# The last stage of a fused attention and GLU kernel: more output buffers, two kinds of transfers on another queue, one output more added in DRAM

## Chip, core and metric

The kernel runs on one core of a Trainium2 chip. The metric is device time in microseconds: the median of 3 runs before the change is 725.43 us (724.59 to 726.86). All times below are in us unless they say otherwise.

## What is computed

```python
def _A_ref(x, wqkv, wo):                 # x: 1 x 2048 x 640
    q, k, v = ...                        # 32 heads of 20
    phi = lambda t: jnp.where(t > 0, t + 1, jnp.exp(t)) + 1e-6
    pq, pk = phi(q), phi(k)
    kv = jnp.einsum("bhsd,bhse->bhde", pk, v)
    z = jnp.einsum("bhsd->bhd", pk)
    num = jnp.einsum("bhqd,bhde->bhqe", pq, kv)
    den = jnp.einsum("bhqd,bhd->bhq", pq, z)[..., None] + 1e-6
    return (num / den, heads put side by side) @ wo

def _B_ref(x, w_gate, w_up, w_down):     # 640 -> 1536 -> 640
    return (sigmoid(x @ w_gate) * (x @ w_up)) @ w_down

g = sigmoid((x * gate_w).sum(-1, keepdims=True))
out = g * _A_ref(...) + (1 - g) * _B_ref(...)
```

Everything is float32, and the output is written transposed, as `out_t`, 640 x 2048.

## The kernel before

Float32 products are made of three matmuls each: an operand is split into a high part (a ScalarE copy, rounded) and a low part (a VectorE subtraction), and high x high, high x low and low x high are added in PSUM (`prod`, `mm3`, `split`).

Linear attention lets kv and wo be folded into one 640 x 640 matrix **M**. What is left for the last stage is `out_t = M^T . pq`, with pq scaled by g / den in each column, plus b, the GLU part times (1 - g). The stage works on five row blocks of 128 (`o`, 0 to 4) and four column groups of 512 (`g`), in the order 2, 3, 0, 1. Groups 2 and 3 are **stage 0** (`n = 0`), groups 0 and 1 **stage 1** (`n = 1`). For groups 2 and 3 b was written to `out_t` before, so the attention part is added to it by a DMA with an addition, which GpSimd's queue alone issues. For groups 0 and 1 b lies in SBUF (`tb`, `BL`), not yet multiplied by (1 - g).

In each stage there are two `ABlock`s (here block 0 and block 1). One computes two row blocks of both groups with seven products in place of eight, as in Strassen's scheme: steps s1 to s7, emitted in the order s1, s2 of both blocks, the fifth row block by itself (`a_unit`), then s3, s4, s5, s7, s6 of block 0 and the same of block 1. Four of M's sums that a block needs (`MS`) are loaded by `load_ms`: for block 0 into one tile (`ws`), for block 1 into two (`wg`), in eight DMAs. Pre-added inputs are the `pt` tiles, and the corrections for the fifth row of inputs lie in `ws`.

The results leave through buffers that are taken in turn by `st_tile` from the list `ST`. A step copies PSUM into a buffer on ScalarE (c11 in s1, c12 in s3, c22 in s4, one more in s6), VectorE adds a second PSUM tile to it (c11 after s2, c22 after s5, c12 after s7), and a DMA writes or adds it to `out_t`. The `ch` PSUM tile of a block goes through s1, s3, s5 and s6; s3 is copied out and s5 goes on adding in the same tile. `ST` has six buffers before: columns 2 and 3 of `fac`, one `wu` tile, `tt` (a tile of the tag `t`), `OMG[2]`, `tt`. A buffer comes round at the seventh call; then the copy waits for the DMA that read it.

What fixes the order: `Order` is a planner that runs while the program is built. It keeps estimates of when TensorE, ScalarE and VectorE are done, and places work waiting in its lists between the matmuls when it fits. Its result is a fixed order on each engine. `Ring` (`sp` for SyncE's queue, `gp` for GpSimd's) estimates DMA landings for it and issues them. On the chip each engine goes through its own list in order; GpSimd and SyncE each use eight semaphores in turn for their DMAs, so the ninth waits for the first to land.

`queue_b_scale(g, os_, store)` multiplies rows of b by (1 - g); rows in `store` are then written to `out_t`, and the attention part is added to them by `more` later. Rows not stored are added up in SBUF by `to_b` and written once. `acc` says which of a block's two rows go by `more`: (c12 and s6's) and (c22).

Of the kernel before, what the change touches and what calls it, by code (L numbers as in the profile page):

```python
# [10 lines left out]
OP = mybir.AluOpType  # L11
# [338 lines left out]
class Ring:  # L350
# [16 lines left out]
    def dma_start(self, out, src, **kw):  # L367
        o = self.order
        start = max(self.t, o.data(out, [src]))
        self.t = start + self.issue  # L370
        (r1, n), (r2, _) = (self.run(ap, 0 if getattr(ap.tensor, "_space", DRAM) == DRAM else 1) for ap in (out, src))
        r = min(r1, r2)
        took = 1.25 * max(1, n // r) * (7 + 0.0377 * r) / 16e3
        self.cell = self.rings.issue(self.n, start + self.lag, took)
        o.put(out, [src], self.cell)
        return self.engine.dma_start(out, src, **kw)  # L376

P_LAG, A_LAG, V_LAG = 0.2, 0.18, 0.14

# [7 lines left out]
def gated_mix_kernel(ctx: ExitStack, tc: tile.TileContext, x0, xt, xn, wk, wv, wo, wst_q, wst_f, out_t):  # L387
# [8 lines left out]
    sp, gp = Ring(nc.sync, order, rings, 0, 0.38, 1.5), Ring(nc.gpsimd, order, rings, 1, 0.55, 2.2)  # L396
# [80 lines left out]
    fac = fac_tile()  # L477
# [597 lines left out]
    g = GTBatch(0, [0])  # L1075
# [8 lines left out]
    for c in range(1, 4):  # L1084
        ck = chunks[c]
        if c == 1:
# [14 lines left out]
            g = GTBatch(c, batches[c])  # L1101
# [98 lines left out]
        if c > 1:  # L1200
            g = GTBatch(c, batches[c])
# [53 lines left out]
    def tt(name, dt=F32, shape=(P, TG)):  # L1255
        return pw.tile(list(shape), dt, name=name, tag="t", bufs=4)

    def ct(name, dt=F32, shape=(P, TG)):
        return pw.tile(list(shape), dt, name=name, tag="c", bufs=5)
# [838 lines left out]
    def h_tile(dt=F32R, i=None):  # L2098

        if i is not None:  # L2100
            pass
        elif "h" not in turn:
            i = 0
        else:
            i = (0, 0, 0, 0, 1, 1, 1, 2)[turn["h"] % 8]
            turn["h"] += 1
        pool = pw2 if i == 2 and len(down_pool) < 3 else down_pool[i]
        return pool.tile([P, 2, TG], dt, name="hf", tag=f"hf{i}", bufs=(4, 3, 1)[i])
# [28 lines left out]
    def h_due(p, name):  # L2137
        seg = {"T1": 1, "B22": 1, "T2": 2, "T3": 2, "T4": 3}[name]
        return {"stream": ("h", p), "due": order.due((order_pr[0], 2 * p + 3, 3 if name == "B22" else f"d{seg}"))}
# [15 lines left out]
    def tail_s(f, blk):  # L2155
# [21 lines left out]
        def t5():  # L2177
# [4 lines left out]
            sub(t4, t4, HR[p, "T2"])  # L2182
            HR[p, "T3"] = t3 = HR[p, "B22"]
            b12 = HR.pop((p, "B12"))
# [13 lines left out]
    OMG = {}  # L2198
# [81 lines left out]
    def down_pair(pr, p):  # L2280
# [31 lines left out]
        d.out("Z1", 3, 1)  # L2312
        d.go("X0", "S3", "T3")
        d.out("X0", 1, 1)
        d.go("X1", "S3", "T3", q=1)
        d.out("X1", 3, 1)
# [29 lines left out]
    def down_last(tail):  # L2346
# [43 lines left out]
        d.out("Z1", 3, 1)  # L2390
        d.go("X0", "S3", "T3")
        d.out("X0", 1, 1)
        d.go("X1", "S3", "T3", q=1)
        d.out("X1", 3, 1)
# [308 lines left out]
    q = q_phase(1, lambda k: [(b12h[:, k], b12l[:, k])], extra)  # L2703
# [32 lines left out]
    q = q_phase(0, lambda k: [tuple(t[:, k] for t in b12)], {0: [lambda: next(down), more_c], 1: [lambda: next(down)], 8: [lambda: order.need((nx[1], 6), False), early_omg], 9: [lambda: queue_ds(LAST), lambda: queue_df(LAST)], 10: [lambda: queue_last("T2", "T3", "T4")]})  # L2736
# [3 lines left out]
    PL, PQ, BL, MHL, PT, MS, X3, ST = {}, {}, {}, {}, {}, {}, [], []  # L2740

    def x2_tile(name="pl", dt=F32):
        return px.tile([P, 2, TG], dt, name=name, tag="x2", bufs=10)
# [30 lines left out]
    def load_ms(i):  # L2774

        t = [ws_tile().rearrange("p a b -> p (a b)")] if i == 0 else [wg_tile().rearrange("p a b -> p (a b)") for _ in range(2)]
        n, q = ((4, sp), (2, gp))[i]
        cs = slice(2 * i * P, 2 * (i + 1) * P)
        at = 4 * n * P

        def view(c, k):
            return t[c][:, k * P:(k + 1) * P]
        for c in range(len(t)):
            w = 4 if i == 0 else 1
            for k in range(0, n, w):
                q.dma_start(f32(t[c][:, 4 * k * P:4 * (k + w) * P].rearrange("p (j c) -> p j c", c=2 * P)),
                             ms_dram[:, n * c + k:n * c + k + w].rearrange("p u j c -> p (u j) c")[:, :, cs])
            for k in range(n):
                u = n * c + k
                for h, f in enumerate(("a11", "a21") if u < 2 else ("a12", "a22")):  # L2790
                    MS[i, f, u % 2] = [view(c, 4 * k + 2 * n + h) for n in range(2)]
        room = (t[0][:, at:at + 2 * P], t[1][:, at:at + 2 * P] if i else MS["spare"])
        for e, o in (("u", (1, 2)), ("d", (0, 3))):
            dst = room[e == "u"]
            for k in range(2):
                q.dma_start(f32(dst[:, k * P:(k + 1) * P]), m5_dram[:, o[k], i * P:(i + 1) * P])
            MS[i, e] = [dst[:, k * P:(k + 1) * P] for k in range(2)]
# [139 lines left out]
    def queue_b_scale(g, os_, store=()):  # L2937
        def fn(o):
            vec2(BL[g][o], BL[g][o], OMG[g], OP.mult)
            if o in store:  # L2940
                gp.dma_start(rows(g, o), BL[g][o])
        for o in os_:
            order.add(0, v_cost(TG), lambda o=o: fn(o), ("b", g, o), lambda o=o: b_at(g, o))

    def rows(g, o, c0=0, c1=TG):
        return out_t[o * P:(o + 1) * P, g * TG + c0:g * TG + c1]

    def a_unit(g, o, cuts=(0, TG)):

        os_ = slice(o * P, (o + 1) * P)  # L2950
        if g < 2:
            order.need(("b", g, o))
        dst = BL[g][o] if g < 2 else st_tile()
        for c0, c1 in zip(cuts, cuts[1:]):
            ps = ps_tile("rot") if g > 1 else SEED.pop((g, o, c0) if (g, o, c0) in SEED else (g, o))
            prod(ps[:, c0:c1], [(MHL[k, 0][:, os_], MHL[k, 1][:, os_], PQ[g][k][0][:, c0:c1],
                                 PQ[g][k][1][:, c0:c1]) for k in range(KC)], g > 1)
            if len(cuts) > 2:
                ch = c0 + P if c1 == TG else c1
                vec_copy(dst[:, c0:ch], ps[:, c0:ch], "p")  # L2960
                if ch < c1:
                    act(dst[:, ch:c1], ps[:, ch:c1], AF.Copy, "p")
                    nc.scalar.dma_start(rows(g, o, ch, c1), dst[:, ch:c1])
                sp.dma_start(rows(g, o, c0, ch), dst[:, c0:ch])
                continue
            act(dst, ps, AF.Copy, "p")
            if g > 1:
                gp.dma_start(rows(g, o), dst, accum_op=OP.add)
            else:
                sp.dma_start(rows(g, o), dst)  # L2970

    class ABlock(Block):
        def __init__(self, i, n):
            self.o = (2 * i, 2 * i + 1)
            self.i, self.n, self.at = i, n, 1e9
            self.acc = [n == 0 or i == 0, n == 0 or i == 0]
            self.ga, self.gb = groups[2 * n:2 * n + 2]

        def w(self, i, c):
# [14 lines left out]
        def out(self, j, g, src):  # L2994
            if self.n:
                sp.dma_start(rows(g, self.o[j]), src)
            else:
                gp.dma_start(rows(g, self.o[j]), src, accum_op=OP.add)

        def more(self, j, g, src):  # L3000
            if self.n:
                order.need(("b", g, self.o[j]))
            gp.dma_start(rows(g, self.o[j]), src, accum_op=OP.add)

        def to_b(self, j, g, src, after="p", last=False):

# [104 lines left out]
    for g in range(2):  # L3111
        BL[g] = {o: tb[:, o, g] for o in range(KC)}
    load_ms(0)
    T3 = [h_tile() for _ in range(2)]
    last_down(0, range(2 * KC))
    load_p(0)
    load_p(1)
    ST += [fac[:, 2], fac[:, 3], f32(wu_tile()).rearrange("p a b -> p (a b)")[:, :TG], lambda: tt("st"),
           OMG[2], lambda: tt("st")]
    blocks = [[ABlock(i, n) for i in range(2)] for n in range(2)]  # L3120
    queue_pt(0)
    for b in blocks[0]:
# [16 lines left out]
    def rest(n, hooks={}):  # L3139
        for i in range(2):  # L3140
            for s in (3, 4, 5, 7, 6):
                getattr(blocks[n][i], f"s{s}")()
                for fn in hooks.get((i, s), ()):
                    fn()
                order.fill()
# [6 lines left out]

    def queue_later():

        order.need(("c11", 0))
        for g, o, tag in ((0, 0, "dd"), (0, 2, "dd"), (0, 4, "rot")):
            queue_seed(g, o, tag)
        queue_pt(1)
        queue_b_scale(1, (0, 1), (0, 1))
        queue_b_scale(0, (1,), (1,))  # L3160

    def queue_end():

        order.add(0, 2 * v_cost(TG // 2), seed_parts, ("b", 1, KC - 1))
        queue_b_scale(1, (2, 3))
        queue_b_scale(0, (3,))
    rest(0, {(0, 6): [lambda: load_omg(0), lambda: load_omg(1)], (1, 4): [queue_later]})
    firsts(1)
    for u in range(KC):
        order.need(("pq", 1, u))  # L3170
    rest(1, {(0, 6): [queue_end]})
    order.need("late")
    a_unit(1, KC - 1, (0, TG // 2, TG))
# [40 lines left out]
```

## Time and profile before

| what | value |
|---|---|
| median of 3 runs | 725.43 us (724.59 to 726.86) |
| profiled execution: time, span | 724.84 us, 722.8 us |
| mean TensorE clock granted | 0.997 |
| TensorE busy, 560 to 660 | 100.00 of 100 |
| TensorE busy, 660 to 680 | 18.92 of 20.00 |
| TensorE busy, 680 to 700 | 18.94 of 20.00, clock 0.91 |
| TensorE busy, 700 to 710 | 10.00 of 10.00 |
| TensorE busy, 710 to the end of the span | 9.07 |
| DMA moved over the whole span | 187.03 MB, mean 259 GB/s |

The span is that of the profiled execution, from its first to its last instruction; its own time is 2.0 us more. The profile shows instructions with start, duration and, in brackets, how long the engine stood idle ahead of them and what ended that. Names are those of the tiles without their numbers. In a row of the view by stretches stand the stretch, its length, each engine's busy time with its instructions, the granted clock, the share of time that the 16 DMA engines were busy, and GB/s; a row with one engine's column has that engine's alone. In a row of DMAs stand what moves, the queue, how many, KB each, and the median time from issue to landing. In a row of waits stand the waiter, whom it waited for, the time in all, how often and the longest.

### The profile page before, as it was taken

The numbers are of one execution on the slowest core, as the hardware profiler recorded it, in microseconds if no ns is written. First come the engines' busy times: TensorE is split into PE (matmuls) and PEld (weight loads), VectorE is DVE, ScalarE is ACT, GpSimd is POOL, SyncE is SP. The second block draws the span as 40 slices with busy tenths as digits, with TensorE's granted clock in tenths as the row PEclk, the third lists the DMA queues.
The fourth block names the chain that finished last, engine by engine and source line by source line (L and its number), as shares of the span: only waits on it lengthen the run. The fifth ranks groups of instructions, "written<-read, shape, count | busy, mean of one in ns | idle before, by whom it ended". The sixth has DMA issues, their size and how long they took to land.

```text
span 722.8 us, 10177 instructions
## 1 busy us (share of the span) xinstructions
PE 715.9 (99%) x3386; PEld 604.2 (84%) x3386; DVE 583.1 (81%) x1051; ACT 375.4 (52%) x720; POOL 202.9 (28%) x337
## 2 busy tenths in 40 slices
PE   9999999999999999999999999999999999999897
PEld 8999999888888888878888888888888888888786
DVE  4988878987887889789978887547778878689895
ACT  5764748257656673746465862464333333336351
POOL 0311111113433434343522123023421413514402
PEclk9999999999999999999999999999999999999999
DMA  8474558699885969598979788996988897997836
GB/s 272 121 199 115 174 140 265 145 315 296 311 309 215 350 189 337 183 351 286 321 239 329 244 260 281 332 347 220 352 298 298 288 368 272 356 331 219 186 59 174
DMA packets 74985, 187.03 MB, mean 259 GB/s; under 512 B 13930, under 2 KB 27898, under 8 KB 74166
## 3 DMA queue, kind: packets, MB, share of 16 engines
q1 hardware_dynamic: 45510, 97.41, 40.1%
q0 software_dynamic: 29136, 88.77, 39.6%
q8 instruction: 26, 0.43, 0.2%
q10 hardware_dynamic: 288, 0.23, 0.1%
q14 instruction: 25, 0.20, 0.1%
HBM read 105.01 MB, written 76.38 MB: 251 GB/s over the span
## 4 chain that ended last, share of the span: by engine, by line
PE 93%; DMA 3%; issue 2%; DVE 1%; ACT 1%; POOL 0%; POOLq 0%; ACTq 0%
PE ch L419 10%; PE ch L421 10%; PE ch L420 10%; PE cc L421 7%; PE cc L420 7%; PE cc L419 7%; PE dd L419 6%; PE dd L421 6%; PE dd L420 6%; PE rot L419 5%; PE rot L421 5%; PE rot L420 5%; PE ch L430 4%; PE cc L430 3%; PE dd L430 2%
## 5 line engine op out<-in xcount | busy, mean ns | idle before, releaser
L439 DVE TENSOR_TENSOR hf<-c,hf 128x512 fp32r<-128x512 f32 x77 | 52.4, 688 | 30.7 <-ACT hf L435 30.5
L435 ACT ACTIVATE hf<-c 128x512 fp32r<-128x512 f32 (+1 forms) x79 | 48.7, 625 | 37.8 <-DVE c L439 37.8
L435 ACT ACTIVATE c<-ch 128x512 f32<-128x512 f32 x43 | 25.7, 597 | 78.7 <-PE ch L430 62.5
L439 DVE TENSOR_TENSOR c<-cc,c 128x512 f32<-128x512 f32 x38 | 26.1, 688 | 26.1 <-ACT c L435 15.2
L439 DVE TENSOR_TENSOR tb<-rot,tb 128x512 f32<-128x512 f32 x60 | 39.0, 683 | 2.9 <-PE rot L421 2.9
L419 PE MATMUL ch<-xth,ws 128*128 128x512 f32 x94 | 36.8, 391 | 0.0
L421 PE MATMUL ch<-xth,ws 128*128 128x512 f32 x94 | 36.6, 390 | 0.0
L420 PE MATMUL ch<-xtl,ws 128*128 128x512 f32 x94 | 36.6, 389 | 0.0
L439 DVE TENSOR_TENSOR c<-c,c 128x512 f32<-128x512 f32 x48 | 33.0, 687 | 2.6 <-ACT c L435 2.0
L435 ACT ACTIVATE dd<-ch 128x512 f32<-128x512 f32 x22 | 12.8, 583 | 38.2 <-PE ch L430 38.2
L376 POOL DMA_DIRECT2D b_dram<-tb x24 | 20.4, 945 | 33.2 <-ACT tb L435 32.9
L435 ACT ACTIVATE c<-dd 128x512 f32<-128x512 f32 x21 | 12.5, 596 | 31.8 <-PE dd L430 30.3
L376 POOL DMA_DIRECT2D zacc<-kr x8 | 7.0, 870 | 77.2 <-DVE logit L845 59.4
L439 DVE TENSOR_TENSOR wst<-wst 128x256 f32<-128x256 f32 (+2 forms) x69 | 27.4, 412 | 1.5
L419 PE MATMUL dd<-xrh,wg 128*128 128x512 f32 x62 | 24.5, 395 | 0.0
L439 DVE TENSOR_TENSOR tb<-dd,tb 128x512 f32<-128x512 f32 x32 | 21.9, 685 | 3.0 <-PE dd L421 3.0
L421 PE MATMUL dd<-xrh,wg 128*128 128x512 f32 x62 | 24.2, 390 | 0.0
L420 PE MATMUL dd<-xrl,wg 128*128 128x512 f32 x62 | 24.1, 390 | 0.0
L435 ACT ACTIVATE c<-c 128x512 f32<-128x512 f32 x31 | 19.5, 628 | 8.1 <-DVE c L439 7.9
L419 PE MATMUL cc<-xbh,ws 128*128 128x512 f32 x58 | 22.6, 389 | 0.0
L420 PE MATMUL cc<-xbl,ws 128*128 128x512 f32 x58 | 22.6, 389 | 0.0
L421 PE MATMUL cc<-xbh,ws 128*128 128x512 f32 x58 | 22.6, 389 | 0.0
(807 smaller groups left out, 2539.2 us busy)
## 6 DMA issues: line engine op xcount, KB each, us to landing
wst<-wst_f SPq DMA_DIRECT2D x12, 640.0 KB, 6.8
wf<-wg POOLq DMA_DIRECT2D x12, 640.0 KB, 4.4
wg<-wf SPq DMA_DIRECT2D x12, 640.0 KB, 8.2
b_dram<-tb POOLq DMA_DIRECT2D x24, 256.0 KB, 6.9
xnst<-xn SPq DMA_DIRECT2D x16, 320.0 KB, 4.2
xst<-xt SPq DMA_DIRECT2D x8, 640.0 KB, 5.9
wp<-ws POOLq DMA_DIRECT2D x20, 256.0 KB, 5.8
wp<-ws POOLq DMA_DIRECT2D x10, 512.0 KB, 4.3
```

The source lines that it names most:

```text
L376: return self.engine.dma_start(out, src, **kw)
L419: nc.tensor.matmul(out, l_hi, r_hi, start=first, stop=False, skip_group_check=True)
L420: nc.tensor.matmul(out, l_hi, r_lo, start=False, stop=False, skip_group_check=True)
L421: nc.tensor.matmul(out, l_lo, r_hi, start=False, stop=last, skip_group_check=True)
L430: nc.tensor.matmul(out, w, x, start=False, stop=n == len(singles) - 1, skip_group_check=True)
L435: nc.scalar.activation(out, src, fn, **kw)
L439: nc.vector.tensor_tensor(out, a, b, op=op)
```

## The change

Six things change, all in the last stage.

1. `ST` holds nine buffers in stage 0: two halves of an `x2` tile and a `c` tile are added, and the order of the list is another. Before stage 1 the three are taken out of the list (`queue_later`), and columns 0 and 1 of `fac` are put at its head: eight buffers.
2. The eight loads of M's sums for block 1 (`load_ms(1)`) go from GpSimd's to SyncE's queue.
3. Rows of b that `queue_b_scale` stores go from GpSimd's to SyncE's queue.
4. `acc` of stage 1's block 1 becomes (no, yes): its c22 of group 1 is no longer copied and added to b in SBUF (`to_b`). VectorE adds s5's `ch` to the buffer, and a DMA adds that to `out_t`.
5. Therefore row 3 of b in group 1 is stored, and scaled ahead of row 2.
6. `add_start` issues the adding DMAs with estimates of their own (0.95 to issue, 4.0 to land) for the planner.

```diff
+    def add_start(self, out, src):
+        was = self.issue, self.lag
+        self.issue, self.lag = 0.95, 4.0
+        self.dma_start(out, src, accum_op=mybir.AluOpType.add)
+        self.issue, self.lag = was
...
-        n, q = ((4, sp), (2, gp))[i]
+        n, q = (4, 2)[i], sp
...
             if o in store:
-                gp.dma_start(rows(g, o), BL[g][o])
+                sp.dma_start(rows(g, o), BL[g][o])
...
             if g > 1:
-                gp.dma_start(rows(g, o), dst, accum_op=OP.add)
+                gp.add_start(rows(g, o), dst)
...
-            self.acc = [n == 0 or i == 0, n == 0 or i == 0]
+            self.acc = [n == 0 or i == 0, True]
...
+    more_st = [x2_tile("st"), ct("st")]
...
     ST += [fac[:, 2], fac[:, 3], f32(wu_tile()).rearrange("p a b -> p (a b)")[:, :TG], lambda: tt("st"),
-           OMG[2], lambda: tt("st")]
+           more_st[0][:, 0], OMG[2], more_st[0][:, 1], lambda: tt("st"), more_st[1]]
+    first_st = (more_st[0].tensor.name, more_st[1].tensor.name)
...
+        ST[:] = [t for t in ST if callable(t) or t.tensor.name not in first_st]
...
-        queue_b_scale(1, (2, 3))
+        queue_b_scale(1, (3, 2), (3,))
...
+    ST[:0] = [fac[:, 0], fac[:, 1]]
     rest(1, {(0, 6): [queue_end]})
```

The calls of `gp.dma_start` with an addition in `out` and `more` become `gp.add_start` as well. The matmuls and their order stay as they are.

ScalarE, from the copy of group 3's fifth row block on (`st_6449`, `st_6451`). `ch1` and `cc1` are block 0's PSUM tiles, `ch0` and `cc0` block 1's, `hf` and `pq` high parts of splits. Before:

```order
L435 ACTIVATE st_6449<-rot1_6450 128x512
L435 ACTIVATE hf_6237<-pl_6125 128x512
L435 ACTIVATE omg_5913<-ch1_6357 128x512
L435 ACTIVATE hf_6237<-pl_6126 128x512
L435 ACTIVATE st_6500<-cc1_6491 128x512
L435 ACTIVATE fac_4701<-ch1_6357 128x512
L435 ACTIVATE fac_4701<-ch0_6371 128x512
L435 ACTIVATE pq_6568<-hf_6344 128x512
L435 ACTIVATE pq_6569<-hf_6344 128x512
L435 ACTIVATE wu_6356<-cc0_6556 128x512
```

And now, where `st_6237` and `st_6238` are the added tiles:

```order
L441 ACTIVATE st_6451<-rot1_6452 128x512
L441 ACTIVATE hf_6239<-pl_6125 128x512
L441 ACTIVATE st_6237<-ch1_6359 128x512
L441 ACTIVATE hf_6239<-pl_6126 128x512
L441 ACTIVATE omg_5913<-cc1_6493 128x512
L441 ACTIVATE st_6237<-ch1_6359 128x512
L441 ACTIVATE st_6555<-ch0_6373 128x512
L441 ACTIVATE pq_6570<-hf_6346 128x512
L441 ACTIVATE pq_6571<-hf_6346 128x512
L441 ACTIVATE pq_6572<-hf_6348 128x512
L441 ACTIVATE st_6238<-cc0_6558 128x512
```

The order of the copies is nearly the same; their targets are others, and one split (`pq`) has moved ahead of block 1's c22 copy.

GpSimd, from group 2's fifth row block on, to the end of stage 0. Before:

```order
L376 DMA out_t<-wu_6356 128x512
L376 DMA wg_6439<-ms_dram_76 128x2x256 x2
L376 DMA wg_6440<-ms_dram_76 128x2x256 x2
L376 DMA wg_6440<-m5_dram_77 128x128 x2
L376 DMA wg_6439<-m5_dram_77 128x128 x2
L376 DMA out_t<-st_6449 128x512
L376 DMA out_t<-fac_4701 128x512 x2
L376 DMA out_t<-st_6500 128x512
L376 DMA out_t<-omg_5913 128x512
L376 DMA out_t<-fac_4701 128x512
```

And now, to the end of the program (the row of three is block 1's s6 of stage 0 and the first two adds of stage 1; two more follow):

```order
L376 DMA out_t<-wu_6358 128x512
L376 DMA out_t<-st_6451 128x512
L376 DMA out_t<-fac_4701 128x512 x2
L376 DMA out_t<-omg_5913 128x512
L376 DMA out_t<-st_6237 128x512 x2
L376 DMA out_t<-st_6238 128x512
L376 DMA out_t<-st_6555 128x512
L376 DMA out_t<-fac_4701 128x512 x3
L376 DMA out_t<-st_6451 128x512
L376 DMA out_t<-st_6555 128x512
```

The loads into `wg` are gone from between the adds; GpSimd now issues adds alone. The last row is the added one.

VectorE, from the last scaling of pq's inputs on (`hf<-hf,fac`). `dd` and `rot` are seeds, products of b and (1 - g) that are put into PSUM. Before:

```order
L443 SCALAR_TENSOR_TENSOR hf_6354<-hf_6354,fac_4701 128x512
L439 TENSOR_TENSOR pq_6568<-hf_6344,pq_6568 128x512
L439 TENSOR_TENSOR pq_6569<-hf_6344,pq_6569 128x512
L439 TENSOR_TENSOR dd0_6585<-tb_2136,omg_6543 128x512
L439 TENSOR_TENSOR dd1_6587<-tb_2136,omg_6543 128x512
L439 TENSOR_TENSOR wu_6356<-ch0_6371,wu_6356 128x512
L439 TENSOR_TENSOR rot0_6599<-tb_2136,omg_6543 128x512
L439 TENSOR_TENSOR pq_6570<-hf_6346,pq_6570 128x512
L439 TENSOR_TENSOR fac_4701<-cc0_6556,fac_4701 128x512
L439 TENSOR_TENSOR pq_6571<-hf_6346,pq_6571 128x512
L439 TENSOR_TENSOR pq_6572<-hf_6348,pq_6572 128x512
```

And now:

```order
L449 SCALAR_TENSOR_TENSOR hf_6356<-hf_6356,fac_4701 128x512
L445 TENSOR_TENSOR pq_6570<-hf_6346,pq_6570 128x512
L445 TENSOR_TENSOR pq_6571<-hf_6346,pq_6571 128x512
L445 TENSOR_TENSOR pq_6572<-hf_6348,pq_6572 128x512
L445 TENSOR_TENSOR dd0_6589<-tb_2136,omg_6544 128x512
L445 TENSOR_TENSOR st_6238<-ch0_6373,st_6238 128x512
L445 TENSOR_TENSOR dd1_6601<-tb_2136,omg_6544 128x512
L445 TENSOR_TENSOR rot0_6603<-tb_2136,omg_6544 128x512
L445 TENSOR_TENSOR st_6555<-cc0_6558,st_6555 128x512
L445 TENSOR_TENSOR pq_6573<-hf_6348,pq_6573 128x512
L445 TENSOR_TENSOR pq_6574<-hf_6350,pq_6574 128x512
```

The addition of s5's `ch` stays fifth after the scaling, now behind three low parts and one seed where there were two of each; two more seeds follow it.

More of the change, by code (lines that the diff above doesn't have):

```diff
@@ L2997, in out @@
             else:
-                gp.dma_start(rows(g, self.o[j]), src, accum_op=OP.add)
+                gp.add_start(rows(g, self.o[j]), src)
         def more(self, j, g, src):
@@ L3002, in more @@
                 order.need(("b", g, self.o[j]))
-            gp.dma_start(rows(g, self.o[j]), src, accum_op=OP.add)
+            gp.add_start(rows(g, self.o[j]), src)
         def to_b(self, j, g, src, after="p", last=False):
```

## The prediction

> **What bounds the kernel now.** I read the page's busy times first, then TensorE's waits, then the timelines of the stretch in which it waits.
>
> ```profile
> PE 715.9 (99%) x3386; PEld 604.2 (84%) x3386; DVE 583.1 (81%) x1051; ACT 375.4 (52%) x720; POOL 202.9 (28%) x337
> PE ch L419 <- ACT fac L435: 2.1, 1, 2.1
> PE rot L530 <- PEq L3205: 0.8, 1, 0.8
> PE rot L419 <- DVE tb L439: 0.2, 1, 0.2
> ```
>
> TensorE is busy 99% of the span. The change adds and removes no matmul, so it can win only where TensorE waits or runs slowly, or behind its last matmul. TensorE has three waits in the whole span. The 0.8 us is the program's start; the one that matters is 2.1 us in `ch`, on a ScalarE copy into `fac`. TensorE's timeline around it (start, duration; the bracket is idle time and releaser):
>
> ```profile
> 675.36 0.39 PE L419 MATMUL ch<-pt,wg 128*128 128x512 f32 x1
> ...
> 676.72 0.39 PE L430 MATMUL ch<-ws,wg 128*128 128x512 f32 x1
> ...
> 678.53 0.39 PE L430 MATMUL cc<-ws,wg 128*128 128x512 f32 x1
> 681.06 0.80 PE L419 MATMUL ch<-pt,wg 128*128 128x512 f32 x1 [2.14 <-ACT fac L435]
> ...
> 684.71 0.39 PE L421 MATMUL cc<-pq,wg 128*128 128x512 f32 x1
> 681.00:684.70 3.70, 3.64 (x9) 0.56 0.74 120
> ```
>
> The last row is of another view, busy time by stretch: after the wait the granted clock is 0.56 for 3.7 us. At full clock matmuls start 0.226 apart (676.72 to 678.53 is 8 steps). So the place costs more than its wait. From 678.53 to 684.71 there are 10 steps: at full clock the tenth starts at 678.53 + 2.26 = 680.79. It starts at 684.71. **The place costs 3.9 us**: 2.3 standing still (678.76 to 681.06) and 1.6 at the low clock.
>
> The matmul at 681.06 is the first of s5 of block 1 of stage 0. It adds into the PSUM tile that ScalarE must first copy out as `c12`. ScalarE's and GpSimd's timelines:
>
> ```profile
> 679.11 0.60 ACT L435 ACTIVATE fac<-ch 128x512 f32<-128x512 f32 x1 [8.12 <-DMA out_t<-fac]
> 680.41 0.60 ACT L435 ACTIVATE fac<-ch 128x512 f32<-128x512 f32 x1 [0.70 <-DMA out_t<-fac]
> 664.44 0.92 POOL L376 DMA_DIRECT2D out_t<-wu  x1 [7.59 <-ACT wu L435]
> 665.15 3.11 POOL L376 DMA_DIRECT2D wg<-ms_dram  x4
> 667.99 2.42 POOL L376 DMA_DIRECT2D wg<-m_dram  x4
> 671.87 0.90 POOL L376 DMA_DIRECT2D out_t<-st  x1 [1.47 <-DMA wg<-ms_dram]
> 672.52 2.00 POOL L376 DMA_DIRECT2D out_t<-fac  x2
> ```
>
> The copy at 680.41 is that `c12`. Its data had been ready since 676.72 + 0.39 = 677.11, but its buffer, a column of `fac`, still held the first result of block 1, which GpSimd's adding DMA had not finished reading. The copy before it waited for the other column. Those adds were issued at 672.52 behind eight loads of M's sums.
>
> **The change, part by part.** With nine buffers, block 0's copies (c12, c22, s6) and block 1's c12 and c22 go to buffers not used in this stage yet; `fac` columns 2 and 3 come round only for block 1's s6 and stage 1's first copy. So both waits go. c12 of block 1 runs at 677.14 to 677.74, 1.0 us ahead of 678.76 when its matmul is due; c22 (`cc`, last matmul done 678.53 + 0.39 = 678.92) stands behind three splits of about 0.5 each and is through by 679.8, ahead of s7, due at 678.76 + 7 x 0.226 = 680.35.
>
> What is late next? From 678.76 on all of TensorE's work is due 3.9 us earlier, so whatever feeds it must follow. VectorE is the narrow one:
>
> ```profile
> 674.49 4.30 DVE L443 SCALAR_TENSOR_TENSOR hf<-hf,fac 128x512 f32<-128x512 f32 x7
> 681.56 1.29 DVE L439 TENSOR_TENSOR pq<-hf,pq 128x512 fp32r<-128x512 f32 x2 [2.77 <-ACT pq L435]
> 688.14 0.60 ACT L435 ACTIVATE st<-ch 128x512 f32<-128x512 f32 x1 [3.54 <-issue]
> 690.17 1.15 ACT L435 ACTIVATE pq<-hf 128x512 fp32r<-128x512 f32 x2
> ```
>
> Its operations start 0.60 apart (seven take 4.30). It is free at 678.7 whatever the change does, and its 2.77 us of idling, which waited for ScalarE, goes too. In the new order stand three `pq`, one seed, then the add of s5's `ch`: start 678.7 + 4 x 0.60 = 681.1, end 681.8. TensorE's s6, which reuses that `ch`, is due at 678.76 + 15 x 0.226 = 682.15. **Margin 0.3 us**, the smallest of all. Next: `pq` of row block 4 is five operations later (start 684.1, end 684.8), and s1 of stage 1 needs its low half at its seventh matmul, 682.15 + 8 x 0.226 + 6 x 0.226 = 685.3: margin 0.5. ScalarE, which stood idle 3.54 us ahead of 688.14, copies block 1's s6 from 684.2; from there all three engines run as before, 3.9 us earlier.
>
> The new buffers have a price: two of them lie where stage 1's last `pq` tile goes, so that split (before, the second of the two that begin at 690.17; now due about 690.7 - 3.9 = 686.8) waits for the adds of c12 and s6 of block 0. The second is issued after its copy, 676.2. The landings:
>
> ```profile
> 647.57 6.10 SPq L376 DMA_DIRECT2D hf<-p_dram  x6
> out_t<-fac POOLq DMA_DIRECT2D x6, 256.0 KB, 5.0
> out_t<-omg POOLq DMA_DIRECT2D x1, 256.0 KB, 8.0
> wg<-ms_dram POOLq DMA_DIRECT2D x4, 256.0 KB, 6.1
> hf<-p_dram SPq DMA_DIRECT2D x4, 512.0 KB, 8.4
> out_t<-tb SPq DMA_DIRECT2D x4, 256.0 KB, 2.3
> 676.00:684.00 8.00, 5.86 (x20) 4.44 (x20) 5.23 (x9) 4.19 (x9) 1.10 (x2) 0.80 0.98 161
> 660.00:665.00 5.00, 5.00 (x24) 4.14 (x23) 4.87 (x9) 3.74 (x7) 0.56 (x1) 1.00 0.14 41
> ```
>
> Even the longest landing, 8.0, gives 684.2: in time by 2.6, so nothing is charged.
>
> M's sums on SyncE's queue: eight DMAs go behind `hf<-p_dram` there. Those were issued until 653.7, and each sums load waits for the DMA eight places ahead to land, 653.7 + 8.4 = 662 at the latest; the DMAs are nearly empty then (share 0.14 from 660 to 665). With 6.1 us they are in by 669, and TensorE needs the first at 675.36. Behind them on SyncE stand only the two gate loads, first needed at 680.5. GpSimd loses 5.5 us of issuing in front of the adds: block 1's first add goes at 671.6, when VectorE has made it, not 673.1. Cost nothing, cover 6 us.
>
> **The end.** The last matmul, VectorE's and ScalarE's copies and the last small DMAs are as before and follow TensorE, 3.9 us earlier:
>
> ```profile
> 718.79 0.28 PE L421 MATMUL rot<-pq,wf 128*128 128x256 f32 x1
> 709.46 0.69 DVE L439 TENSOR_TENSOR tb<-tb,omg 128x512 f32<-128x512 f32 x1
> 706.17 1.16 POOL L376 DMA_DIRECT2D out_t<-tb  x2 [15.78 <-DVE tb L439]
> 717.00 0.85 POOL L376 DMA_DIRECT2D out_t<-wu  x1 [4.85 <-issue]
> 719.74 0.35 ACTq L2963 DMA_DIRECT2D out_t<-tb  x1
> 702.00:709.00 7.00, 7.00 (x33) 5.72 (x32) 6.90 (x13) 2.59 (x5) 1.13 (x2) 1.00 0.18 75
> 709.00:717.00 8.00, 8.00 (x44) 6.91 (x43) 5.71 (x10) 1.33 (x3) 2.32 (x3) 1.00 0.88 228
> 717.00:722.80 5.80, 2.07 (x18) 1.87 (x16) 0.72 (x2) 0.28 (x1) 0.85 (x1) 0.92 0.58 137
> ```
>
> Before, three rows of b go by GpSimd (from 706.17), and the last add leaves only at 717.00, since the store it adds to stood behind two adds. Now the four stores leave SyncE from about 706.17 - 3.9 = 702.3 to 706.2 (the fourth stands where VectorE's row at 709.46 stood, 705.6 plus 0.69) and land 2.3 later, so the first three adds leave at about 705 to 707 and the fourth at 708.7. The fourth's sum is now one VectorE addition out of `ch`, where ScalarE copied and VectorE added; s7's eight matmuls, 1.8 us, lie between s5 and s6, which needs that `ch`, and the addition needs 0.2 + 0.69 of them: margin 0.9. The DMAs work 1.3 + 7.0 + 3.4 = 11.7 us after 702; one add more costs about 2 (five adds filled the engines some 10 us up to 683), so 13.7, and from 702 to the new end, 718.9, there are 16.9. At 5.0 to 8.0 after 708.7 the last add is in by 713.7 to 716.7. I take nothing, with 0 to 1 as bounds.
>
> **Sum.** 724.84 (the profiled execution's own time; its span is 722.8) - 3.9 = 720.9. That execution lies 0.6 below the median of 725.43, inside their 724.59 to 726.86. If the others' extra lies in this wait, it goes too: 720.9. If it lies elsewhere, 721.5. I forecast **721.2**, its own range 720.0 to 722.2.
>
> The Trainium skill speaks against part of this: "TensorE: Matmul & The Clock Gate", section "What's actually happening", has the clock halve after at least one idle window of about 3.4 us. This gap was 2.1 us, and the rows show a slow clock right behind it all the same. By that rule the slow matmuls would have another cause and stay; by the rows they belong to the gap, and I go by the rows.
>
> **Rivals.**
> - *VectorE takes the wait over.* The 0.3 us margin at s6 is eaten by a late operation or two (0.6 to 1.2), and TensorE waits 0.3 to 0.9, perhaps with the slow clock behind it (1.6): 721.5 to 723.7, middle 722.7. For it: VectorE is busy 4.87 of the 5.00 us from 660. Against: it had idle time in exactly this stretch. 0.12.
> - *Only the gap goes, the slow clock stays*: 724.84 - 2.3 = 722.5. For it: 2.1 us is a short gap. Against: the clock is 1.00 elsewhere in the stage. 0.03.
> - *It does not do what it says*: the copies meet another transfer that still holds their buffer, or the late `pq` split waits, and the 3.9 come back: 724.8, within 0.3% of the median (723.3 to 727.6). It would need a landing beyond 10 us from 676.2. 0.09.
> - *The last add ends the program, slower.* If adds on GpSimd's queue, instead of overlapping, each start when the one before has landed, four from 705 at 5.0 end at 725, and the program at about 727.5. It decides once the last lands after 718, and is worse than before from 722.5. Against: the adds issued together at 672.52 released their copies 1.3 apart (679.11, 680.41). The Trainium skill's "DMA: Bandwidth & Descriptors", "Issuing engines are not separate DMA queues", has all queues share the same 16 engines; the trace's shares agree that stores on SyncE and adds on GpSimd are one sum of work, the 13.7 above. 0.06.
>
> **How the numbers follow.** Forecast 0.70, the rivals 0.12, 0.03, 0.09 and 0.06. Faster by over 0.3% (below 723.3; about the least that a measurement can tell) are the forecast, most of the first rival (0.08) and the second: 0.81. Within 0.3%: 0.04 + 0.09 = 0.13. Slower: 0.06. The range, 719.9 to 723.5, takes in the forecast, the first two rivals and the end's bounds.
>
> **What would show it.** No wait of TensorE over 0.3 us after the start; full clock from 676 to 688; `ch` copied at 677.1 without a DMA wait; VectorE's add of s5 done by 681.9; the last matmul's end near 715.2 instead of 719.1; the last GpSimd add issued before 710. The prediction is wrong if the split of the last `pq` tile, or s6 of block 1, shows a new wait, or if the span goes on more than 4 us past the last matmul.

## The result and the profile after

The changed kernel takes **722.16 us** (median of 6 runs, 721.89 to 722.99), the kernel before 725.88 in the runs beside it (6 runs, 724.59 to 728.36): ratio 0.9947, 95% interval 0.9929 to 0.9965. The forecast was 721.2 with a range of 719.9 to 723.5. The profiled execution of the changed kernel took 722.47, its span 720.7; that of before took 724.84, so this pair differs by 2.4, the medians by 3.7. Both differences matter below. One run of the kernel before in the later batches, 763.58 at a mean clock of 0.889, is left out of every figure below.

Read in the order of the prediction. First the page's busy times and TensorE's waits of the changed kernel (in the waits: us in all, times, longest; where a row by stretch has five busy times, they are those of PE, PEld, DVE, ACT and POOL, that is TensorE's matmuls and weight loads, VectorE, ScalarE, GpSimd):

```profile
PE 714.4 (99%) x3386; PEld 604.0 (84%) x3386; DVE 581.9 (81%) x1050; ACT 374.8 (52%) x719; POOL 197.4 (27%) x327
PE rot L536 <- PEq L3216: 0.8, 1, 0.8
PE rot L425 <- DVE tb L445: 0.2, 1, 0.2
```

The wait of 2.1 us is gone and no new one is in its place. TensorE's timeline at that place, and the busy times of the stretch behind it:

```profile
675.62 0.39 PE L425 MATMUL ch<-pt,wg 128*128 128x512 f32 x1
...
676.98 0.39 PE L436 MATMUL ch<-ws,wg 128*128 128x512 f32 x1
...
678.79 0.39 PE L436 MATMUL cc<-ws,wg 128*128 128x512 f32 x1
679.02 0.39 PE L425 MATMUL ch<-pt,wg 128*128 128x512 f32 x1
...
681.00:684.70 3.70, 3.70 (x18) 3.04 (x18) 3.70 (x7) 0.88 (x3) 1.39 (x2) 1.00 0.37 47
```

s5 of block 1 follows its forerunner by 0.23, and 18 matmuls instead of 9 run in the stretch, at clock 1.00. This execution came to the stage 0.26 later than the profiled one of before (675.62 against 675.36). Two executions of the kernel before differ by more at this matmul (675.36, and 674.85 in experiment 6), so nothing is read from that. Then ScalarE, VectorE, GpSimd and SyncE around the stage:

```profile
677.40 0.60 ACT L441 ACTIVATE st<-ch 128x512 f32<-128x512 f32 x1 [0.99 <-PE ch L436]
679.46 0.58 ACT L441 ACTIVATE st<-cc 128x512 f32<-128x512 f32 x1
678.96 1.88 DVE L445 TENSOR_TENSOR pq<-hf,pq 128x512 fp32r<-128x512 f32 x3
681.37 0.68 DVE L445 TENSOR_TENSOR st<-ch,st 128x512 f32<-128x512 f32 x1
671.53 1.71 POOL L376 DMA_DIRECT2D out_t<-fac  x2 [2.56 <-DVE fac L445]
656.85 4.93 SPq L376 DMA_DIRECT2D wg<-ms_dram  x4
662.78 3.25 SPq L376 DMA_DIRECT2D wg<-m_dram  x4
```

`c12` is copied as its last matmul ends (676.98 + 0.39), without a DMA wait; `c22` at 679.46. VectorE's add of s5 ends at 682.05, and s6 starts at 682.42: the margin was 0.37.

The end is where the forecast misses. The last matmul, GpSimd's last adds, and the DMAs of the end by stretch:

```profile
715.13 0.28 PE L427 MATMUL rot<-pq,wf 128*128 128x256 f32 x1
705.80 1.72 POOL L376 DMA_DIRECT2D out_t<-fac  x2 [19.63 <-DMA out_t<-tb]
706.90 1.51 POOL L376 DMA_DIRECT2D out_t<-st  x1
711.84 0.85 POOL L376 DMA_DIRECT2D out_t<-st  x1 [3.44 <-DMA out_t<-tb]
706.49 9.61 SPq L376 DMA_DIRECT2D out_t<-tb  x5
700.00:705.00 5.00, 5.00 (x24) 4.08 (x23) 5.00 (x9) 1.04 (x3) 0.00 (x0) 1.00 0.30 114
705.00:713.00 8.00, 8.00 (x43) 6.83 (x42) 5.34 (x10) 1.03 (x2) 3.45 (x4) 1.00 1.03 223
713.00:720.70 7.70, 2.41 (x21) 2.21 (x19) 0.72 (x2) 0.28 (x1) 0.00 (x0) 0.96 0.59 139
```

The last matmul starts at 715.13, 3.66 earlier than before's 718.79, or 3.9 counted from the start of the stage. But the program goes on 5.6 us behind it (span 720.75), where the kernel before needed 4.05. **The stage gained 3.9 as forecast, and the end gave 1.6 back.** The last add left at 711.84, not at 708.7, and the row shows why: it waited 3.44 for a store of b (`tb`), the one that SyncE issued at 706.49 and that landed at 711.3. The records of the last instructions show where the end goes (us; the closing drain is GpSimd's last instruction of length; these are single records of the traces):

```
                                before   changed
last matmul starts              718.79   715.13
GpSimd's last DMA has landed    721.31   717.53
GpSimd's closing drain ends     722.05   719.66
SyncE's last wait is over       722.05   718.80
end of the span                 722.84   720.75
```

Before, drain and SyncE ended together. Now the drain ends 0.86 later than SyncE; SyncE's own last wait comes 3.67 after the last matmul instead of 3.26 (0.41 more); and from the later of the two to the span's end it is 1.09 instead of 0.79 (0.30). 0.86 + 0.41 + 0.30 = 1.57.

### The profile page after: what moved, and what is told of

The parts are those of the page before. It is cut to its first block, busy times and chain, and to the rows that moved or that the text cites. A ratio compares the mean times of both kernels' runs of the same rounds, so it can differ in the third digit from the quotient of the medians.

```text
span 720.7 us, 10168 instructions
## 1 busy us (share of the span) xinstructions
PE 714.4 (99%) x3386; PEld 604.0 (84%) x3386; DVE 581.9 (81%) x1050; ACT 374.8 (52%) x719; POOL 197.4 (27%) x327
## 4 chain that ended last, share of the span: by engine, by line
PE 98%; ACT 1%; DVE 0%; issue 0%; ACTq 0%
PE ch L425 10%; PE ch L427 10%; PE ch L426 10%; PE cc L426 7%; PE cc L425 7%; PE cc L427 7%; PE dd L425 6%; PE dd L427 6%; PE dd L426 6%; PE rot L425 6%; PE rot L427 6%; PE rot L426 6%; PE ch L436 4%; PE cc L436 3%; PE dd L436 2%; PE rot L1789 1%
```

## The experiments

Twelve runs in four batches; kernels of one batch ran on the same chip and share the runs of the kernel before. The theory: the buffers take the waits away, the queue of M's sums alone would not have; the low clock belongs to the gap; the end's loss comes of the added add. The rivals: the queue did it; the low clock has another cause; the end's loss is chance.

**1. The queue alone.** The kernel before with M's later sums on SyncE:

```diff
-        n, q = ((4, sp), (2, gp))[i]
+        n, q = (4, 2)[i], sp
```

> Of the change only the loads of M's sums go to SyncE's queue; six buffers, stores of b on GpSimd and the last output summed in SBUF stay as before. Theory A (the adds were late because eight loads stood ahead of them on GpSimd): the first two adds of stage 0 leave near 671.5 and 672.1 in place of 672.5 and 673.1 and land near 676.7 and 678.0, so ScalarE's two copies into fac come 2 us earlier, TensorE's wait of 2.1 us shrinks to 0 to 0.3 and its clock stays full; the last matmul starts 3.6 to 3.9 earlier and the time is near 721.1 to 722. Rival B (only more buffers take the wait away): a wait of 1 us or more stays on a copy into fac, with the slow clock behind it, 723.5 or more.

Measured: 724.40 (722.88 to 725.12, 11 runs; before 725.58), ratio 0.9984 [0.9973, 0.9995]. GpSimd's adds, ScalarE's copies of block 1 and TensorE's waits of this kernel:

```profile
671.34 1.71 POOL L376 DMA_DIRECT2D out_t<-fac  x2 [2.58 <-DVE fac L439]
677.98 0.60 ACT L435 ACTIVATE fac<-ch 128x512 f32<-128x512 f32 x1 [6.92 <-DMA out_t<-fac]
679.28 0.60 ACT L435 ACTIVATE fac<-ch 128x512 f32<-128x512 f32 x1 [0.69 <-DMA out_t<-fac]
PE ch L419 <- ACT fac L435: 0.9, 1, 0.9
PE cc L419 <- ACT wu L435: 0.2, 1, 0.2
```

The adds leave 1.2 earlier (671.34 against 672.52), the copies run 1.1 earlier (679.28 against 680.41), and 1.1 us of waits stay, with the clock at full behind them. From the first matmul of block 1's s3 (675.43 here, 675.36 before) to the last matmul (716.65) this kernel takes 41.2 instead of 43.4, so the stage gained 2.2 of the 3.9. Behind the last matmul it takes 5.9 instead of 4.05: GpSimd's drain ends 2.22 behind the last landing (0.75 before) and 1.37 past SyncE's last wait. The 1.2 of the medians is what is left of the one after the other; experiments 8 and 9 come back to the drain.

**2. The buffers alone.** The changed kernel with three parts as they were: M's sums and the stores of b on GpSimd, and no added add.

```diff
-        n, q = (4, 2)[i], sp
+        n, q = ((4, sp), (2, gp))[i]
-                sp.dma_start(rows(g, o), BL[g][o])
+                gp.dma_start(rows(g, o), BL[g][o])
-            self.acc = [n == 0 or i == 0, True]
+            self.acc = [n == 0 or i == 0, n == 0 or i == 0]
-        queue_b_scale(1, (3, 2), (3,))
+        queue_b_scale(1, (2, 3))
```

> Of the change only the buffers (nine in stage 0, eight in stage 1) and the planner's estimates for adds; the loads of M's sums and the stores of b stay on GpSimd's queue, the last output is summed in SBUF. Theory A (a buffer that nobody holds needs no early add): no wait of TensorE in stage 0 though the first adds still leave at 672.5 and land at 679 to 680.3; the last matmul 3.6 to 3.9 earlier than before, time near 721 to 722. Rival B (later adds hold the last pq tile, or the buffers of stage 1): a wait of 0.5 us or more on ScalarE's last pq split or on a copy of stage 1, 722.5 or more.

Measured: 720.69 (719.80 to 722.72, 6 runs), ratio 0.9934 [0.9919, 0.9950]. GpSimd's adds and ScalarE's copy `c12`:

```profile
673.56 2.00 POOL L376 DMA_DIRECT2D out_t<-fac  x2
678.06 0.60 ACT L441 ACTIVATE st<-ch 128x512 f32<-128x512 f32 x1 [0.99 <-PE ch L436]
```

The adds leave 2.0 later than in the changed kernel and land at 680.06 and 681.35, yet the copy waits for TensorE alone, and from s3 to the last matmul it is 39.5, as in the changed kernel. The buffers, with the planner's estimates for adds, which this kernel keeps and no run takes apart from them, do the whole of it. By the medians this kernel is also faster than the changed one (722.27 in this batch, experiment 4), though its own runs spread from 719.80 to 722.72.

**3. Without the added add.** The changed kernel with the last two edits of experiment 2 alone.

> The changed kernel without its added DRAM addition: c22 of block 1 in stage 1 is copied and summed in SBUF again, row 3 of b in group 1 is not stored, rows 2 and 3 are scaled in the old order. Theory A (GpSimd's closing drain, which begins after its last add at 711.84 and ends at 719.66, holds the end of the program 0.9 us past SyncE's last wait at 718.80): the last add leaves near 707, the drain ends before SyncE is done, and the time is 0.7 to 1.5 us under the changed kernel's, span near 719.5. Rival B (the end is set by the last small outputs and the closing steps whatever GpSimd does): within 0.3 us of the changed kernel.

**4. The changed kernel again, beside them.**

> The changed kernel once more, on the same chip as its parts, as their measure: 721.9 to 723.0, no wait of TensorE in the last stage, GpSimd's closing drain about 0.9 us past SyncE's last wait. If the drain's excess comes and goes between executions of one kernel, it will differ here by more than 0.5 us.

Measured: 720.16 (720.01 to 720.45, 5 runs), ratio 0.9925 [0.9911, 0.9939], against 722.27 (721.61 to 723.22, 5 runs), ratio 0.9954 [0.9937, 0.9971]: 2.1 us for one DMA of 256 KB, more than the 0.7 to 1.5 that was expected. GpSimd's last adds and the end by stretch without it:

```profile
704.95 1.72 POOL L376 DMA_DIRECT2D out_t<-fac  x2 [19.65 <-DVE rot L445]
706.05 1.51 POOL L376 DMA_DIRECT2D out_t<-st  x1
705.00:713.00 8.00, 8.00 (x46) 6.99 (x45) 5.36 (x10) 1.20 (x2) 2.56 (x3) 1.00 1.03 192
713.00:718.00 5.00, 1.57 (x14) 1.37 (x12) 0.53 (x2) 0.28 (x1) 0.00 (x0) 0.99 0.41 140
```

The DMA engines are as full up to 713 and emptier behind. The drain ends at 715.18, ahead of SyncE's last wait (717.38), and the span ends 4.16 after the last matmul (5.63 in the run of the changed kernel beside it). That accounts for 1.5 of the 2.1. The other 0.6 lies ahead of the last stage, where TensorE's instructions are the same in both: s3 came at 674.75 here and at 675.39 in the changed kernel beside it. Whether that is chance isn't shown.

**5. The gap filled.** Does the slow clock belong to the gap? The kernel before, TensorE busied while it would stand:

```diff
+            if self.n == 0 and self.i == 1:
+                fill, (w, _, xh, _) = ps_borrow("rot"), self.xb(1, 2, 4)
+                for k in range(9):
+                    nc.tensor.matmul(fill, w, xh, start=True, stop=True, skip_group_check=True)
```

> The kernel before with nine more matmuls of TensorE (512 columns each, 0.23 us apiece, 2.1 us together, into a tile of PSUM that nothing reads) put just ahead of the products of block 1 that waited. Nothing else is changed: the adds of c11, and the ScalarE copies that wait for their landing, stand where they stood. Theory A (the slow clock behind the wait belongs to TensorE's standing still): TensorE is busy up to about 681, stands 0.3 us or less, and the 18 matmuls of s5 that took 3.7 us run at full clock, in about the time of the same count elsewhere in the stage (0.22 us each, 4 us for 18 against 5.6): 1.2 to 1.6 us under the kernel before. Rival B (the slow clock comes of something else at that time, such as the load on the chip): the matmuls of s5 run as slow as before, and the time is that of before within 0.5 us, or above it by what of the filling doesn't fit.

**6. The kernel before once more, for one profile.**

> The kernel before once more, for its profile alone. Both theories on the slow clock (that a gap of 2.1 us brings it, or that it is of another cause) look at the same rows: the wait of TensorE ahead of s5 of block 1 and the spacing of the 18 matmuls behind it. If the gap brings it, a gap of about 2 us shows the same 0.3 to 0.4 us spacing behind it again.

Measured: 5 takes 723.33 (722.48 to 725.44, 12 runs; before 724.63 there), ratio 0.9988 [0.9976, 0.9999]. TensorE's timeline and the stretch behind, first with the gap filled, then in the second profile of the kernel before:

```profile
678.61 2.20 PE L3067 MATMUL rot<-pq,wf 128*128 128x512 f32 x9
680.86 0.50 PE L419 MATMUL ch<-pt,wg 128*128 128x512 f32 x1
...
681.00:684.70 3.70, 3.70 (x16) 2.79 (x17) 3.34 (x6) 3.41 (x7) 0.19 (x1) 1.00 0.70 110
```

```profile
678.03 0.39 PE L430 MATMUL cc<-ws,wg 128*128 128x512 f32 x1
681.11 0.50 PE L419 MATMUL ch<-pt,wg 128*128 128x512 f32 x1 [2.70 <-ACT fac L435]
681.45 0.40 PE L420 MATMUL ch<-pt,wg 128*128 128x512 f32 x1
...
681.00:684.70 3.70, 3.59 (x15) 2.74 (x15) 3.09 (x6) 3.66 (x8) 0.00 (x0) 1.00 0.63 102
```

The second fence is the surprise. TensorE stood longer here (2.70 instead of 2.14), and the clock behind is 1.00: this execution of before took 723.71. So the slow stretch comes in some executions and not in others. In its place, by steps of 3.41 us and TensorE alone, first in the profile of before that the prediction used, then in this one:

```profile
677.46:680.87 3.41, 1.46 (x7) 1.00 1.11 196
680.87:684.28 3.41, 3.22 (x8) 0.50 0.85 139
```

```profile
676.89:680.30 3.41, 1.52 (x7) 1.00 1.04 172
680.30:683.71 3.41, 2.60 (x11) 1.00 0.89 149
```

The clock was halved for exactly one such step. In each of the 14 profiles the clock's records change only whole multiples of 3.413 us after the clock first rises: here 198 of them, from 5.03 to 680.87. In the second profile it rose at 4.46, and the steps counted from there cut the gap at 680.30.

How often does the slow stretch come? 3.7 us at 0.56 lower the mean clock of a whole execution by 0.002, which the result of each run shows (0.997 in before's profiled one). The runs of before in the four batches, by that mean:

```
mean clock         0.999 or 1.000     0.998     0.997 or less
runs of 75         31                 10        34
mean time, us      723.1              725.1     725.6
```

With the gap filled, 11 of 12 runs have 0.999 or more; of the 17 of before beside them 8 have. Of the 89 runs of all kernels in which TensorE doesn't stand here (experiment 5, the changed kernel, 2 to 4 and 7 to 12) none has 0.997 or less; of the 11 of experiment 1, which stands for 1.1, 2 have. (A mean of 0.998 can come of the end alone: in experiment 4's profile the low clock begins at 717.29, behind the last matmul.) So the slow clock belongs to the gap, and the 11 runs with the gap filled take 723.2 in the mean, as before's full-clock runs do (723.1): theory A, with a size that depends on how often. The low clock itself costs 1.6 in the one profile that has it; the rest of the 2.5 between the table's first and last row isn't traced. Why a gap of 2.1 brought it once and one of 2.7 did not is open. The Trainium skill's "TensorE: Matmul & The Clock Gate", "What's actually happening", has the activity window of the gate run free of the program, so that the place of a gap in it would differ between executions. The steps of 3.413 agree with that. But that window of about 3.4 us is longer than both gaps, so neither held a whole idle one, and the two steps ahead were about equally busy (1.46 and 1.52 of 3.41); no run here moved a gap against the window.

**7. The fastest, with M's sums back on GpSimd.** Experiment 3 with the first edit of experiment 2:

> The fastest run so far (the changed kernel with one output less added by a DRAM transfer) with one thing more undone: M's later sums go to GpSimd's queue again, so that of the queue part only the stores of b's rows are left on SyncE. Theory A (with the buffers in turn no copy waits for the adds any more, so the queue of M's sums is worth nothing here): the adds of c11 leave at about 673.5 and land at 680 to 681.4 as in the run with buffers alone, no wait of TensorE in the stage, and the time is within 0.3 us of the run without the last add. Rival B (the queue gives something of its own): slower than that run by 0.5 us or more, as the run with buffers alone, which differs from this one in the stores of b's rows alone, was 0.5 us above it.

Measured: 720.28 (719.89 to 721.38, 6 runs), no wait of TensorE in the stage. Within 0.3 of experiment 3, in another batch: with the buffers there, the queue of M's sums is worth nothing. What the stores of b on SyncE bring lies between nothing and the 0.5 between experiments 2 and 3, whose ranges overlap.

**8 and 9. The closing drain.** How far behind the landing of GpSimd's last DMA the drain ends, in the profiles so far and those of the same kernels in the last batch, by the number of GpSimd's DMAs in the trace:

```
DMAs on GpSimd   kernel                                   drain ends behind last landing, us
326              before (twice), 2, 5                     0.74, 0.75, 0.75, 0.75
323              7                                        0.62
318              1                                        2.22
316              changed (three times)                    2.13, 2.13, 2.14
315              3 (twice)                                2.10, 2.10
```

Is it the count? Experiment 8 is the changed kernel with M's sums (eight loads) back on GpSimd. Experiment 9 leaves them on SyncE and gives GpSimd eight other DMAs that nothing reads:

```diff
+    idle_dram = dram.tile([P, 8, P], F32, name="idle_dram")
...
+    for k in range(8):
+        gp.dma_start(idle_dram[:, k], m5_dram[:, k % 4, :P])
```

> The changed kernel with M's later sums back on GpSimd's queue (eight loads), all else as changed. In the seven kernels profiled that keep a late add or have the eight loads on either queue, GpSimd's closing drain ends 0.6 to 0.75 us behind the landing of its last DMA where the loads are on GpSimd, and 2.1 to 2.2 us behind it where they are on SyncE. Theory A (taking the eight DMAs off GpSimd's queue makes its closing drain longer): the drain ends 0.75 us behind the last add's landing (about 718.3 instead of 719.7, behind SyncE's last wait or level with it), no copy waits in the stage, and the time is 0.8 to 1.2 us under the changed kernel (about 721.2). Rival B (the long drain comes of the late add among the stores, and the loads' queue has nothing to do with it): the drain ends 2.1 us behind the landing, and the time is that of the changed kernel within 0.3 us.

> The changed kernel (M's sums on SyncE) with eight other DMAs on GpSimd's queue, 64 KB each from one scratch tensor in DRAM to another that nothing reads, in a stretch of the last stage in which the DMA engines are nearly idle. The computation is that of the changed kernel. Theory A1 (the drain depends on the number of DMAs on GpSimd's queue, or on where its ring then stands): the drain ends 0.75 us behind the last landing as in the kernels with 323 or 326 DMAs on that queue, and the time is 0.8 to 1.2 us under the changed kernel. Theory A2 (it depends on these loads themselves, or on another thing): the drain ends 2.1 us behind, and the time is that of the changed kernel, or up to 0.5 us above it for the traffic.

Measured: 721.48 (720.89 to 722.37, 12 runs), ratio 0.9968 [0.9954, 0.9982], and 721.31 (720.60 to 722.09, 12 runs), ratio 0.9957 [0.9941, 0.9973]. The drain ends 0.67 and 0.50 behind the last landing, and 0.49 and 1.59 ahead of SyncE's last wait; the span ends 4.6 after the last matmul in both, against 5.6. So it is not these loads: eight other DMAs bring the drain's end as near to the landing. Whether the count counts, or where the queue then stands in some ring, wasn't tried. As ratios the two don't beat the changed kernel's 0.9947, for the batches of before differ in how many runs have the slow clock. So the three were run side by side.

**10 to 12. The changed kernel, experiment 8 and experiment 3 in one batch.**

> The changed kernel again, on the same chip as the next two, since its ratio to the kernel before depends on how many of the latter's executions have the slow clock. Expected: its closing drain 2.1 us behind the last add's landing, time 722.2 within 0.4. Theory A (count of GpSimd's DMAs lengthens the drain and the last add costs time of its own): it is the slowest of the three.

> The changed kernel with M's later sums on GpSimd's queue, beside the changed kernel on one chip. Theory A (the drain is 1.4 us shorter and was 0.86 past SyncE's last wait): 0.8 to 1.2 us under the changed kernel. Rival B (what the drain gives back is lost elsewhere, and the lower time of the run before was its chip's): within 0.3 us of it.

> The changed kernel without the one output more that is added by a DRAM transfer, beside the changed kernel on one chip. Theory A (the added add costs its drain and emptier DMA engines, some 2 us): 1.5 to 2.3 us under the changed kernel. Rival B (the 2.1 us of the first run was the chance of a few executions): 0.5 to 1.2 us under it.

```
                         us (runs)      lowest, highest    ratio to before, interval
changed                  722.59 (12)    721.53, 722.99     0.9973 [0.9960, 0.9986]
sums back on GpSimd      720.99 (7)     720.59, 722.02     0.9953 [0.9933, 0.9973]
without the added add    720.53 (6)     719.88, 721.21     0.9941 [0.9922, 0.9961]
```

Both orders hold: M's sums on SyncE cost the changed kernel 1.6 here (0.8 by the medians of the batches before; the span beyond the last matmul shrinks from 5.2 to 4.5, so the profiled pair bears out 0.8), and the added add costs 2.1. Of that the profiles put 1.1 at the end (the span beyond the last matmul is 4.15 without the add) and 0.7 ahead of the last stage (s3 at 674.62 and 675.33), again with no cause known. The two effects overlap: with no late add the drain ends early and its length is hidden. The added add leaves at 711.62 in this run of the changed kernel, and its drain ends at 719.02, 0.84 past SyncE's last wait.

## Why the prediction was right, and where it was not

- **The place costs 3.9 (2.3 standing, 1.6 at the low clock): right for that execution, and the stage gave exactly that back.** It is not the cost of every execution. In the second profile the gap was larger and the low clock absent; over all batches the kernel before takes 723.1 in the mean with the full clock, and the change gains 0.7 (the changed kernel's 23 runs have the median 722.4); where the low clock comes (725.6), it gains 3.2. The forecast said nothing of this; it took one profile's stretch as given.
- **The buffers take both waits away: right.** Experiment 2 shows it alone; by experiment 1 the queue without the buffers leaves 1.1 us of waits. (Block 1's first add left at 672.52 before; the prediction's 673.1 is the second, 673.13.)
- **VectorE is narrowest at s6, margin 0.3: right** (0.37). The rival that VectorE takes over did not come. No split of the last `pq` tile waited: the second add of block 0, issued 676.71, landed at 682.27, ahead of 686.8.
- **M's sums on SyncE are in by 669 and cost nothing: the first half about right** (the last landed at 670.6, still ahead of 675.36), **the second wrong**, and for a reason that the prediction didn't look at: with eight DMAs fewer on GpSimd's queue its closing drain ends 1.4 later behind the last landing (2.13 against 0.75), which shows as soon as a late add puts the drain last.
- **The end, "I take nothing, with 0 to 1 as bounds": this is the step that failed.** It measured 1.6 in the profiled pair; taking the added add out again gives 1.5 and 1.1 at the end of the profiles, and 2.1 in the medians. The prediction let the fourth store land 2.3 after its issue, the duration of a store on empty engines. Four stores and three adds already filled the DMAs (share 1.03 from 705 to 713), and the fourth, issued at 706.49, took 4.79; so its add left 3.1 late and landed at 717.53 instead of 713.7 to 716.7. GpSimd's drain behind it, which ended 0.86 past SyncE's last wait, was not in the sum at all. The DMAs' work from 700 on, 5.0 x 0.30 + 8.0 x 1.03 + 7.7 x 0.59 = 14.3 us, was near the 13.7 of the forecast: the amount was right, and it said nothing about when the last of it would land. The prediction had named a span of more than 4 us beyond the last matmul as the sign of its being wrong, and that sign came: 5.6. It was drawn too tight, since the kernel before already took 4.05; the sign that tells is the other one, the last add issued before 710, which failed with 711.84.
- **The rival "the last add ends the program"** is the nearest to what happened, by another mechanism: the adds did overlap (the first three landed at 711.0, 712.6 and 714.4), but the drain behind the last of them ended the program, and the end cost 1.6 and not 6.
- **The rival "only the gap goes, the slow clock stays": not so**; by experiment 5 the slow clock goes with the gap. Nor did the change fail to do what it says: no copy met a transfer that still held its buffer.
- **The sum.** 724.84 - 3.9 + 1.6 for the end is 722.5, the changed kernel's profiled execution (722.47); two smaller differences cancel in it, 0.26 later at the stage and 0.28 less outside the span. The forecast stood 1.0 under the median and not 1.6, since it had put 0.3 on for the other runs, and the median lies 0.3 under the profiled execution. That its own range, 720.0 to 722.2, still holds the median of 722.16 is luck: the end went 0.6 past its bounds of 0 to 1, and the two 0.3, which come of the choice of runs and not of the mechanism, made up for it.

The run that beats both kernels is the changed one without the added add: 720.16 and 720.53 in two batches, 2.1 us under the changed kernel in each.

## What to carry to other kernels

When a wait is removed near a program's end, write the end's chain down to the last instruction of every engine, closing drains too, and take the landing of a DMA from a row with the same load on the engines, not from an idle stretch. Look at a slow stretch in more than one execution before its time is put into a sum. An output written by a transfer instead of an engine is cheap only where the engines that move it have time left behind it.

## What the runs showed that was not expected

- GpSimd's closing drain took 5.1 to 9.3 us and ended 0.5 to 0.75 behind the last landing in kernels with 323 DMAs or more on its queue, and 2.1 to 2.2 behind it with 318 or fewer, in 14 profiles without an exception; eight idle DMAs of 64 KB took its end from 2.13 to 0.50 behind the landing.
- The clock behind one gap was low in about half of the executions of one and the same program (34 of 75 by the mean clock), which took 2.5 us more in the means; it came in one step of 3.41 us at half clock.
- The executions of one kernel drift apart in their first 50 us: the same VectorE operations came about 1.0 us earlier in experiment 4's profile than in the changed kernel's first one from 53 us to 399, and 0.23 earlier from 427 to the last stage. The first lead goes with the clock: in the one TensorE's matmuls start 0.15 apart from 4.7 on, in the other 0.27 apart up to 6.6. In the five profiles in which the clock first rises by 4.52, one VectorE operation stands at 64.6, and in the nine in which it rises at 5.0 to 6.7, at 64.9 to 65.7. Stretches can be compared between two profiles; whole spans differ by this chance.
